# Moving the bias-row transposes and the gelu table load in a one-core Trainium2 kernel (gated mix of an SSM convolution and a token-mixing MLP)

## The chip, the cores and the metric

One core of a Trainium2 chip. The metric is the device time of one execution in microseconds (us); lower is better. The time before is the median of three runs. TensorE (PE) does the matmuls into PSUM, ScalarE (ACT) and VectorE (DVE) read PSUM and work on SBUF, GpSimd (POOL) and SyncE (SP) issue most of the DMAs.

## The reference

Two branches over S = 2048 positions and D = 640 channels, mixed by a gate per position. All inputs are bf16.

```python
x = A_q
g = sigmoid((x * gate_w).sum(-1, keepdims=True))
# a: a short causal convolution of k (4 taps a channel), times v; then a long causal
#    convolution over S with ssm_k, by FFT; plus the skip ssm_D; times q
kv = shift(k, shift_k) * v
a = x * (irfft(rfft(kv_padded) * rfft(ssm_k_padded))[:S] + kv * ssm_D)
# b: layernorm over D, then an MLP over the positions
h = layernorm(B-branch input x)
u = gelu(einsum("bsd,sf->bdf", h, w1) + b1)      # F = 1536
b = (einsum("bdf,fs->bds", u, w2) + b2).T
return g * a + (1 - g) * b
```

## The kernel before

The long convolution is done as matmuls with a 128x128 transform: `FTB` holds its cosine and sine tables, made at the start from integer ramps by ScalarE's sine. The whole kernel is one list of operations that `_Sched` gathers. `_Sched.add` finds what each operation depends on from the memory regions that it reads and writes; `_Sched.run` simulates the engines with a duration for each operation and a rate for each DMA, and from that picks the order on each engine and which of the four PSUM buffers (`pp`, each 1024 fp32 a partition) every group of matmuls takes; `emit` writes the operations out in that order. `_Tracker` puts in the semaphore waits. Every PSUM group is filled by TensorE (line 298) and drained by a step of another engine, nearly always ScalarE (`act`, line 676); the buffer is free for the next group when the drain has ended.

The stages that matter here, in order:

- **wtr / wT.** The SSM kernel rows (`ssm`) are turned by TensorE, eight 128x128 transposes to a buffer (five buffers for each half of the sequence), and drained into `wT`. In the first half, matmuls on a block of zeros (`zz`) stand between them.
- **W.** The transform of `wT`: groups of matmuls `pp<-wT,FTB` with 320 columns, drained to `C`. The first half has sixteen groups of four; the second begins with eight groups of two (`fwd_even`).
- **cst / cc.** `consts()` turns the rows of the two MLP biases (`rows`, loaded by two small DMAs from `B_b1` and `B_b2`) by five small matmuls against `ident`, and one activation drains them to `cc` (128x28). The gelu steps read their bias from it, and so does a VectorE step much later.
- **layernorm.** VectorE makes the statistics of `X` and scales it tile by tile; between these it copies the loaded rows of k (`kn` to `kp`), which SP's DMA then transposes into `KT`.
- **m1 / gelu.** The inner MLP product, `pp<-X,ring`: for each of 12 column blocks four runs of eight matmuls, drained by `GT <- gelu(pp + bias)`. Two blocks are open at a time; in the order before, the first two blocks' runs lie between the W groups. The first gelu makes ScalarE load another activation table.
- **kv.** The short convolution, `pp<-KF,KT` (matmuls of 128 or 96 columns), drained to `ksh`, multiplied by v on VectorE (`vkv`, `kv`).
- then the transform of kv, the products and mixing on VectorE (`C`, `SS`, `tm`), the rest of m1, the outer product m2 (`pp<-GT,W`), and the inverse transform (`pp<-C,FTB` and `pp<-SS,FTB`) with its drains `cgb`; the result goes out by `O`.

In the order of the profiled program, `cst` comes behind the third of the sixteen W groups, and `cc` behind the drains of two of them.

Of the kernel before, what the change touches and what calls it, by code (L numbers as in the profile page):

```python
# [13 lines left out]
ACT = mybir.ActivationFunctionType  # L14
ALU = mybir.AluOpType

ENGS = ("PE", "ACT", "DVE", "POOL")
# [294 lines left out]


class _Op:
    __slots__ = ("eng", "dur", "emit", "prio", "idx", "ndep", "succ", "vt", "vtrole", "end", "start", "kind", "lat", "deps", "name", "after", "nafter", "asucc", "lock")


class _VT:
# [10 lines left out]
class _Sched:  # L329
# [29 lines left out]
    def add(self, eng, dur, emit, reads, writes, prio=None, vt=None, lat=0.0, name=""):  # L359
        op = _Op()  # L360
        op.eng, op.dur, op.emit, op.lat, op.name = eng, dur, emit, lat, name
        op.idx = len(self.ops)
        op.prio = op.idx if prio is None else prio
        op.vt = vt
        op.lock = eng == "POOL"
        deps = set()
        self._conf(op, reads, "R", deps)
        self._conf(op, writes, "W", deps)
        if vt is not None:
            vt.left += 1  # L370
            if vt.last_pe is not None:
                deps.add(vt.last_pe)
            if eng == "PE":
                if vt.first is None:
                    vt.first = op
                vt.last_pe = op
            else:
                for d in deps:
                    if d.vt is not vt and not vt.keep:
                        if d not in vt.first.deps:  # L380
                            vt.first.deps.add(d)
        op.deps = deps
        op.after = set()
        self._rec(op, reads, "R")
        self._rec(op, writes, "W")
        self.ops.append(op)
        return op

    def run(self):
        ops = self.ops  # L390
        for op in ops:
            op.succ = []
            op.asucc = []
            op.ndep = len(op.deps) + len(op.after)
        for op in ops:
            for d in op.deps:
                d.succ.append(op)
            for d in op.after:
                d.asucc.append(op)
        engs = list(ENGS) + ["SP", "QA"]  # L400
        ready = {e: [] for e in engs}
        pend = {e: [] for e in engs}
        free = {"ACT": 2.93, "DVE": 0.85, "POOL": 0.83, "PE": 1.18, "SP": 0.0, "QA": 0.0}
        port = {"DVE": 0.0, "POOL": 0.0}
        dma_free = 0.3
        avail = {}
        for op in ops:
            avail[op] = 0.0
            if op.ndep == 0:
                heapq.heappush(pend[op.eng], (0.0, op.prio, op.idx))  # L410
        nfree = list(range(self.NSLOT))
        held = {}
        events = []
        order = []
        t = 0.0
        done = 0
        started = 0
        n = len(ops)
        frees = []
        while started < n:  # L420
            while frees and frees[0][0] <= t:
                _, sl, cls = heapq.heappop(frees)
                nfree.append(sl)
                held[cls] -= 1
            nxt = []
            progress = False
            for e in engs:
                while pend[e] and pend[e][0][0] <= t:
                    _, p, i = heapq.heappop(pend[e])
                    heapq.heappush(ready[e], (p, i))  # L430
                if free[e] > t:
                    nxt.append(free[e])
                    continue
                skipped = []
                pick = None
                while ready[e]:
                    p, i = heapq.heappop(ready[e])
                    op = ops[i]
                    if op.vt is not None and op.vt.slot is None:
                        c = op.vt.cls  # L440
                        if not nfree or held.get(c, 0) >= self.limit.get(c, 99):
                            skipped.append((p, i))
                            continue
                    pick = op
                    break
                for s in skipped:
                    heapq.heappush(ready[e], s)
                if pick is None:
                    if pend[e]:
                        nxt.append(pend[e][0][0])  # L450
                    continue
                op = pick
                progress = True
                started += 1
                if op.vt is not None and op.vt.slot is None:
                    op.vt.slot = nfree.pop(0)
                    held[op.vt.cls] = held.get(op.vt.cls, 0) + 1
                op.start = t
                if e in ("SP", "QA") or op.lat < 0:
                    issue = 1.2 if e == "POOL" else 0.1  # L460
                    s = max(t + issue, dma_free)
                    dma_free = s + op.dur
                    op.end = dma_free + 2.0 + (6.0 if e == "POOL" else 0.0)
                    free[e] = t + issue
                else:
                    op.end = t + op.dur
                    if op.lock:
                        op.end += max(port["POOL" if e == "DVE" else "DVE"] - t, 0.0)
                        port[e] = op.end
                    free[e] = op.end  # L470
                order.append(op)
                if op.vt is not None:
                    op.vt.left -= 1
                    if op.vt.left == 0:
                        heapq.heappush(frees, (op.end + 0.05, op.vt.slot, op.vt.cls))
                for s in op.asucc:
                    avail[s] = max(avail[s], op.start)
                    s.ndep -= 1
                    if s.ndep == 0:
                        heapq.heappush(pend[s.eng], (avail[s], s.prio, s.idx))  # L480
                for s in op.succ:
                    lat = 0.08 if s.eng == e else 0.15
                    if e == "PE" and s.eng == "PE":
                        lat = 0.0
                    avail[s] = max(avail[s], op.end + lat)
                    s.ndep -= 1
                    if s.ndep == 0:
                        heapq.heappush(pend[s.eng], (avail[s], s.prio, s.idx))
                nxt.append(free[e])
            if not progress:  # L490
                c = [x for x in nxt if x > t]
                if frees:
                    c.append(frees[0][0])
                assert c, "schedule stuck: " + str([(o.name, o.eng, o.ndep) for o in ops if not hasattr(o, "end")][:12])
                t = min(c)
        self.order = order
        self.makespan = max(o.end for o in ops)
        return order

    def emit(self):  # L500
        for op in self.order:
# [13 lines left out]
def _build(nc, A_q, A_k, A_v, A_shift_k, A_ssm_k, A_ssm_D, B_x, B_w1, B_b1, B_w2, B_b2, gate_w, out):  # L515
    Bsz, S, D = A_q.shape
    F = B_w1.shape[1]
# [8 lines left out]
    with ExitStack() as es:  # L526
# [8 lines left out]
        SC = _Sched(T, pp)  # L535
# [38 lines left out]
        gws = alloc("gws", [128, 1], F32)  # L574
# [64 lines left out]
        def ts(eng, o, a, s1, s2, op0, op1=None, mode=1, prio=None, extra=0.0):  # L639
            n = n_of(o)  # L640
            d = dve_dur(n, mode) + extra if eng == "DVE" else n / 900.0 + 0.2
            rr = [a] + [x for x in (s1, s2) if isinstance(x, bass.AP)]

            def f(e):
                if s2 is None:
                    return e.tensor_scalar(o, a, s1, None, op0=op0)
                return e.tensor_scalar(o, a, s1, s2, op0=op0, op1=op1)
            o_ = SC.add(eng, d, lambda s: T.op(eng, f, rr, [o]), rr, [o], prio=prio, name="ts")
            o_.lock = eng == "POOL" or mode > 1
            return o_  # L650

        def stt(eng, o, a, sc, b, op0, op1, acc=None, prio=None):
# [75 lines left out]
        def dr(t, off, ap):  # L728
            return bass.AP(tensor=t.tensor, offset=t.offset + off, ap=ap)
# [22 lines left out]
            dma(X[:, hk, :, :], dr(A_q, 512 * hk * D, [[4 * D, 128], [1, 4 * D]]), 128 * 5120, chain=True, rate=(352.0 if hk == 0 else 415.0))  # L752

        def w1_load(c, hk):
            dma(ring[c % 2][:, 4 * hk:4 * hk + 4, :], dr(B_w1, 512 * hk * F + 512 * c, [[4 * F, 128], [F, 4], [1, 512]]), 128 * 4096, chain=True)

        def k_load(hk):
            dma(kn[hk % 2][:, :, :], row8(A_k, hk), 128 * 5120, chain=True)
# [213 lines left out]
        for h in range(2):  # L972
            for db in range(ND):
                transp(h, db)
            if h == 0:
                consts()
            if h in (1,):
                fwd_even(srcW(h), h, C[h], 1.0 / 1024.0, h == 1, "W")
            for p in (PORD if h not in (1,) else PORD[2:]):
# [348 lines left out]
        Z1 = invmix(A1[0], A1[1], (SS, 0), False, [z0last])  # L1328
        inverse(1, Z1)

        SC.run()
        SC.emit()
        if _REPORT is not None:
            _REPORT(SC)
        T.wait_dma_final("SP", "out")

    return None


_REPORT = None  # L1340
# [1 line left out]
_INS = ['A_q', 'A_k', 'A_v', 'A_shift_k', 'A_ssm_k', 'A_ssm_D', 'B_x', 'B_w1', 'B_b1', 'B_w2', 'B_b2', 'gate_w']  # L1342
_OUTS = [((1, 2048, 640), 'bfloat16')]
# [23 lines left out]
```

## Time and profile before

| | |
|---|---|
| time, median of 3 runs | 179.74 us (179.69 to 180.02) |
| span of the profiled execution, first to last instruction | 178.7 us; the page lists no other time for it, and the median is 1.04 us above this span |
| TensorE busy | 170.9 us (96%), 1373 matmuls |
| VectorE busy | 169.5 us (95%) |
| ScalarE busy | 117.0 us (65%) |
| GpSimd busy | 43.1 us (24%) |
| mean granted TensorE clock | 0.999 |

"Busy" counts time in which an engine runs a compute instruction. A row of a timeline gives the start, the length from the first start to the last end, the engine and line, the operation, the tile written and the tiles read, shapes, and how many instructions are merged; the bracket is the idle time of that engine just before the row and what ended it. Neighbouring instructions of one engine overlap: a 320-column matmul is listed with about 0.30 us and the next starts 0.136 us after it. One line of the source stands for many places, since each kind of operation is recorded by one helper; the tiles tell them apart.

### The profile page before, as it was taken

What the parts mean: (1) busy time and instruction counts of PE and PEld (TensorE: products, weight loads), DVE (VectorE), ACT (ScalarE), POOL (GpSimd) and SP (SyncE); (2) the same over time, 40 slices, a digit from 0 to 9 for tenths busy, and PEclk for the clock granted to TensorE, in tenths of its full rate; (3) what the DMA queues carried; (4) which work ended last, traced back from release to release, by engine and by line L of the source; (5) the groups of instructions that cost most, each with busy time, mean ns of one, the idle gap of its engine ahead of it and who ended that gap; (6) DMA issues with size and microseconds to landing.
All of it is one profiled execution on the core that took longest, in us unless ns stands there. A gap on an engine that the chain in (4) does not pass through costs nothing.

```text
span 178.7 us, 3326 instructions
## 1 busy us (share of the span) xinstructions
PE 170.9 (96%) x1373; PEld 128.4 (72%) x1374; DVE 169.5 (95%) x203; ACT 117.0 (65%) x176; POOL 43.1 (24%) x52
## 2 busy tenths in 40 slices
PE   7868999899999999999999999999999999999993
PEld 2545787487778677776777778888888887777772
DVE  7799889979999999999999899999999999999984
ACT  4998997999899999428999921131231323753760
POOL 8099803100000065000241100403525000252000
PEclk9999999999999999999999999999999999999999
DMA  5999999999999999999499989797999999599463
GB/s 145 384 413 372 388 301 206 264 421 299 213 258 289 189 272 235 229 229 231 97 244 285 173 132 363 158 229 241 171 194 221 208 201 394 205 164 236 114 233 138
DMA packets 38542, 43.51 MB, mean 243 GB/s; under 512 B 15867, under 2 KB 31360, under 8 KB 38528
## 3 DMA queue, kind: packets, MB, share of 16 engines
q1 hardware_dynamic: 33296, 32.16, 59.1%
q0 software_dynamic: 5200, 11.14, 35.8%
q8 instruction: 11, 0.18, 0.4%
q14 instruction: 3, 0.02, 0.0%
q10 hardware_dynamic: 32, 0.01, 0.0%
HBM read 25.87 MB, written 2.62 MB: 159 GB/s over the span
## 4 chain that ended last, share of the span: by engine, by line
PE 88%; DMA 6%; ACT 3%; SPq 2%; issue 0%; DVE 0%
PE pp L298 88%; DMA rows<-in_B_b_dram 6%; SPq L272 2%; ACT C L676 1%; ACT L676 1%; ACT GT L676 0%; DVE O L688 0%
## 5 line engine op out<-in xcount | busy, mean ns | idle before, releaser
L632 DVE TENSOR_TENSOR C<-C 128x2560 bf16<-128x2560 bf16 (+2 forms) x37 | 54.5, 1525 | 1.1 <-ACT C L676 1.1
L298 PE MATMUL pp<-X,ring 128*128 128x320 bf16 x384 | 55.4, 299 | 0.0
L298 PE MATMUL pp<-GT,W 128*128 128x320 bf16 x384 | 52.6, 299 | 0.0
L298 PEld LDWEIGHTS pp<-GT,W 128*128 128x128 bf16 x384 | 43.6, 114 | 8.6
L298 PEld LDWEIGHTS pp<-X,ring 128*128 128x128 bf16 x384 | 37.3, 98 | 14.3
L676 ACT ACTIVATE C<-pp 128x640 bf16<-128x640 f32 x64 | 40.5, 737 | 3.2 <-PE pp L298 3.2
L676 ACT ACTIVATE O<-pp,c,omg 128x640 bf16<-128x640 f32 x15 | 13.3, 884 | 34.7 <-PE pp L298 34.7
L267 POOL DMA_DIRECT2D C<-C x8 | 11.0, 1615 | 45.0 <-DVE C L632 45.0
L298 PE MATMUL pp<-wT,FTB 128*128 128x320 bf16 x112 | 17.1, 299 | 1.4 <-ACT wT L676 0.8
L676 ACT ACTIVATE cgb<-pp,gg 128x640 bf16<-128x640 f32 x16 | 12.7, 794 | 5.7 <-PE pp L298 5.3
L676 ACT ACTIVATE GT<-pp,cc 128x640 bf16<-128x640 f32 x12 | 9.6, 801 | 9.0 <-PE pp L298 9.0
L298 PEld LDWEIGHTS pp<-wT,FTB 128*128 128x128 bf16 x112 | 10.5, 98 | 6.5 <-ACT wT L676 1.2
L945 DVE BATCH_NORM_STATS2 stats<-X 128x6 f32<-128x320 bf16 x32 | 13.5, 461 | 1.1 <-DMA X<-in_A_q_dram 1.1
L632 DVE TENSOR_TENSOR tm<-C,C 128x2560 bf16<-128x2560 bf16 (+1 forms) x7 | 14.3, 2060 | 0.0
L298 PE MATMUL pp<-C,FTB 128*128 128x320 bf16 x96 | 13.4, 299 | 0.0
L267 POOL DMA_DIRECT2D C<-q_hi x6 | 5.9, 977 | 27.6 <-DVE C L632 13.1
L298 PEld LDWEIGHTS pp<-C,FTB 128*128 128x128 bf16 x96 | 9.3, 98 | 3.8 <-issue 0.2
L676 ACT ACTIVATE gq<-gq 128x640 bf16<-128x640 bf16 x16 | 11.8, 739 | 0.1
L632 DVE TENSOR_TENSOR SS<-C 128x2560 bf16<-128x2560 bf16 x8 | 11.7, 1488 | 0.1
L632 DVE TENSOR_TENSOR C<-tm 128x2560 bf16<-128x2560 bf16 (+1 forms) x9 | 10.7, 1194 | 0.1
L676 ACT ACTIVATE ksh<-pp 128x1024 bf16<-128x1024 f32 (+1 forms) x12 | 9.9, 903 | 0.2 <-PE pp L298 0.2
L676 ACT ACTIVATE wT<-pp 128x1024 bf16<-128x1024 f32 x10 | 9.7, 1027 | 0.6 <-PE pp L298 0.6
(77 smaller groups left out, 188.8 us busy)
## 6 DMA issues: line engine op xcount, KB each, us to landing
ring<-in_B_w_dram SPq DMA_DIRECT2D x12, 512.0 KB, 9.6
W<-in_B_w_dram SPq DMA_DIRECT2D x12, 512.0 KB, 6.3
C<-C POOLq DMA_DIRECT2D x8, 640.0 KB, 10.6
X<-in_A_q_dram SPq DMA_DIRECT2D x4, 640.0 KB, 9.0
kn<-in_A_k_dram SPq DMA_DIRECT2D x4, 640.0 KB, 9.3
out_dram<-O SPq DMA_DIRECT2D x7, 320.0 KB, 3.2
C<-SS POOLq DMA_DIRECT2D x3, 640.0 KB, 11.7
ssm<-in_A_ssm_k_dram SPq DMA_DIRECT2D x3, 512.0 KB, 7.4
```

What stands on the lines that cost most here:

```text
L267: ins = engobj.dma_start(out_ap, in_ap, accum_op=ALU.add, max_dma_last_dim=2560)
L272: ins = engobj.dma_start(out_ap, in_ap)
L298: ins = self.nc.tensor.matmul(ps_ap, lhsT=lhsT, rhs=rhs, start=start, stop=stop, skip_group_check=True)
L632: o_ = SC.add(eng, d, lambda s: T.op(eng, lambda e: e.tensor_tensor(o, a, b, op), rd, [o]), rd, [o], prio=prio, name="tt")
L676: return T.op("ACT", lambda e: e.activation(o, src, func, **kw), rr + [src], ww)
L945: ops.append(SC.add("DVE", 0.38, (lambda o, i: lambda s: T.op("DVE", lambda e: e.bn_stats(o, i), [i], [o]))(o, i), [i], [o]))
```

## The change

The planner's run is taken out. The order of all operations and the PSUM buffer of each group are listed in the source (`_ORDER`, `_SLOTS`), and `follow` sets them. Against the order and buffers that the planner made in the kernel before:

- TensorE: the five `cst` transposes leave their place behind the third W group and stand before the last run of eight m1 matmuls ahead of the second half's W groups, that is between the two m1 runs that follow the last wtr group. Their buffer is the same one, number 1; the group before them in it is now the fourth `wtr` of the second half, the one behind them the first `fwd_even` W group.
- ScalarE: `cc` moves from behind the second drain of W to behind the fifth `wT` drain of the second half. Behind it stands a new activation, a gelu of one column of a constant (`cst[:,1:2]`, −0.5) into `gws`, which is written anew later. The load of the gelu table stands before this new activation, and no longer before the first gelu of the MLP.
- VectorE, GpSimd, SP and the DMAs issued by ScalarE keep their order, and every group keeps its buffer.

The other edits (a `hint` set in place of an added dependency, a DMA rate, a lock flag, the duration given to the new activation) were inputs of the planner.

```diff
-                        if d not in vt.first.deps:
-                            vt.first.deps.add(d)
+                        vt.first.hint.add(d)
...
-    def run(self):
...
+    def follow(self, order, slots):
+
+        vts, done = {}, set()
+        for op in self.ops:
+            if op.vt is not None and id(op.vt) not in vts:
+                vts[id(op.vt)] = op.vt
+        for vt, s in zip(vts.values(), slots):
+            vt.slot = s
+        self.order = [self.ops[i] for i in order]
+        assert len(set(order)) == len(self.ops)
+        for op in self.order:
+            assert all(d.idx in done for d in op.deps)
+            done.add(op.idx)
...
-            o_.lock = eng == "POOL" or mode > 1
+            o_.lock = eng == "POOL"
...
-            dma(ring[c % 2][:, 4 * hk:4 * hk + 4, :], ..., 128 * 4096, chain=True)
+            dma(ring[c % 2][:, 4 * hk:4 * hk + 4, :], ..., 128 * 4096, chain=True, rate=325.0)
...
             if h == 0:
                 consts()
+                act(gws[:, 0:1], cst[:, 1:2], ACT.Gelu_apprx_tanh, name="table").dur = 1.4
...
-        SC.run()
+        SC.follow([int(i) for i in _ORDER.split()], [int(i) for i in _SLOTS])
         SC.emit()
-        if _REPORT is not None:
-            _REPORT(SC)
...
+_ORDER = """
+2 0 3 1 4 5 6 7 8 9 10 18 15 11 12 19 16 13 20 14 17 30 21 33 22 31 23 32 24 36 34 25 26 35 27 57 38 28 37 29 242 39
...
+"""
+_SLOTS = "201301123023102310231021021010101031103103100310331003311023123123312311232302301231231232201230312031203120312031322032032020132013"
```

## The prediction

> **What bounds the kernel now.** I read the page's chain first, then the chain in order of time.
>
> ```profile
> ## 4 chain that ended last, share of the span: by engine, by line
> PE 88%; DMA 6%; ACT 3%; SPq 2%; issue 0%; DVE 0%
> PE pp L298 88%; DMA rows<-in_B_b_dram 6%; SPq L272 2%; ACT C L676 1%; ACT L676 1%; ACT GT L676 0%; DVE O L688 0%
> ```
>
> ```profile
> 4.64 10.14 DMA rows<-in_B_b_dram
> ...
> 14.82 16.34 PE pp L298 x143
> ...
> 32.50 1.28 ACT L676
> ...
> 33.80 0.79 ACT GT L676
> ...
> 35.92 140.11 PE pp L298 x1128
> ```
>
> From 35.92 us on, TensorE runs 1128 matmuls in a row to 176.03, and one VectorE step and one store follow. So the only question is when that run starts. Ahead of it the chain has two foreign pieces: the load of the bias rows, and ScalarE's table load (L676 without a tile) with the first gelu (GT). Both stall TensorE, as its timeline shows (start, length, what, count, idle time before it and what ended it):
>
> ```profile
> 12.47 1.67 PE L298 MATMUL pp<-wT,FTB 128*128 128x320 bf16 x11 [0.77 <-ACT wT L676]
> 14.82 0.38 PE L298 MATMUL pp<-ident,rows 4*128 4x4 bf16 x5 [0.68 <-DMA rows<-in_B_b_dram]
> 15.13 7.24 PE L298 MATMUL pp<-wT,FTB 128*128 128x320 bf16 x52
> ...
> 34.64 1.04 PE L298 MATMUL pp<-wT,FTB 128*128 128x320 bf16 x4 [0.51 <-ACT GT L676]
> 35.92 3.94 PE L298 MATMUL pp<-KF,KT 128*128 128x128 bf16 x72 [0.24 <-ACT C L676]
> ```
>
> ScalarE drains every PSUM buffer; its timeline shows the same stretch:
>
> ```profile
> 13.35 1.29 ACT L676 ACTIVATE C<-pp 128x640 bf16<-128x640 f32 x2
> 15.24 0.19 ACT L676 ACTIVATE cc<-pp 128x28 f32<-128x28 f32 x1 [0.60 <-PE pp L298]
> 15.33 8.45 ACT L676 ACTIVATE C<-pp 128x640 bf16<-128x640 f32 x14
> 23.99 4.69 ACT L676 ACTIVATE wT<-pp 128x1024 bf16<-128x1024 f32 x5 [0.20 <-PE pp L298]
> 29.55 1.30 ACT L676 ACTIVATE C<-pp 128x640 bf16<-128x640 f32 x2 [0.88 <-PE pp L298]
> ...
> 32.50 1.28 ACT L676 ACT_TABLE_LOAD   x1
> ```
>
> Last, two engines that could take over as the bound. GpSimd's copy out of KT (first row) runs as soon as the transpose of the k rows has landed; VectorE (next three) is filled from 37.00 on.
>
> ```profile
> 34.97 1.11 POOL L1079 COPY KT<-KT 128x20 bf16<-128x20 bf16 x1 [4.98 <-DMA KT<-kp]
> ```
>
> ```profile
> 23.91 0.80 DVE L647 TENSOR_SCALAR X<-X,mv,rstd 128x640 bf16<-128x640 bf16 x2
> ...
> 37.00 2.23 DVE L632 TENSOR_TENSOR C<-C 128x1280 bf16<-128x1280 bf16 x2 [1.05 <-ACT C L676]
> 39.37 1.49 DVE L632 TENSOR_TENSOR vkv<-ksh,vkv 128x2560 bf16<-128x2560 bf16 x1
> ```
>
> **The change part by part.** The list keeps every engine's order and every buffer, except this: the five transposes of the bias rows and their drain `cc` leave their place at 14.82 and 15.24. TensorE does the transposes ahead of the last eight matmuls of the X run at 26.90; ScalarE does `cc`, the table load and the tiny gelu behind its five wT drains, ahead of the drains at 29.55. The table load at 32.50 is gone. No DMA is moved, and the queues of SP, GpSimd and VectorE stand as before. Rates and locks are planner figures, which no longer plan anything. I follow TensorE's lead over the trace.
>
> 1. *Stall at 14.82.* The matmul starting at 13.84 is the twelfth; at 0.136 us a step the next could go at 13.98. Its buffer is that of the first W group, whose drain ends at 14.64 − 0.60 = 14.05, so it goes at 14.1. Then ScalarE paces: 14 drains in 8.45 are 0.60 each, four matmuls 0.54. ScalarE's pause of 0.60 and `cc` (0.10 to the next issue) fall away, drain k of the sixteen ends at 14.05 + 0.60(k − 1). The X matmuls at 22.21 use the thirteenth's buffer: 14.05 + 12 × 0.597 = 21.21, so 21.27. **Lead 0.94.** The sixteen drains end at 23.0, not 23.78.
>
> 2. *Second X group (24.78).* Its last two matmuls need the two tiles that VectorE ends at 24.71, and VectorE there waits for a load of k, not for TensorE. The group ends at 25.04 instead of 25.87. **Lead 0.83**, 0.87 at the next X run, where a wait of 0.05 for a wT drain vanishes.
>
> 3. *Transposes.* 14.82 to 15.13, 0.31 us of TensorE, are paid here again: nothing hides them. Their buffer's wT drain has ended by 26.83, before they start at 27.1. The W pair of 29.08 starts at 28.52. **Lead 0.56.**
>
> 4. *Table load.* The wT drains move up 0.94 and end at 27.74 instead of 28.68; `cc` to 27.83, load 1.28 to 29.13, the gelu of 128×1 at most the 0.20 of the 128×16 tanh (100.00). Next drain at 29.25 instead of 29.55. The 1.6 us put in exceed the old pause of 0.88; what pays is the lead of the wT drains. Queued behind it are four drains of W groups, for whose two buffers TensorE waits: the second is free at 30.55, TensorE came at 30.42. It loses 0.13 to 0.2; **lead 0.37**.
>
> 5. *First gelu.* Its matmuls end at 32.1 and no load stands before it: 32.17 to 32.96 instead of 33.80 to 34.59. The two remaining drains that KF×KT waits for end at 34.15; plus the 0.14 seen between drain and matmul at 35.92 it could start at **34.29, lead 1.63**.
>
> 6. *What is late next.* The second matmul of KF×KT reads the k transpose that GpSimd's row shows landed just before 34.97. That load hangs on a copy VectorE makes after a load of k; nothing in it moves. So the run starts effectively at 34.97, against 35.98 for the same matmul: **lead 1.0**, and TensorE rests 0.6 to 0.7 us instead.
>
> 7. *Does the lead last?* VectorE gets its last C drain by 35.4 and could resume at 35.87, ending the pair of 37.00 by 38.10; the next step waits for the third `ksh` drain, which follows KF×KT: 38.35 instead of 39.37. VectorE too gains 1.0. This matters: at 163.91 TensorE takes up C 0.11 us behind its own pace (158.36 + 40 × 0.136 = 163.80) because VectorE has just made it. VectorE's later pause (0.73 at 100.24) hangs on ScalarE, ScalarE on TensorE. Later DMAs all follow one of these engines.
>
> Sum: −1.0 on a span of 178.7. The page gives the span alone; the median, 179.74, is 1.04 above it, for what lies around. 179.74 − 1.0 = **178.74**. Bounds of unknown prices: the gelu of one column between 0 and the 0.29 of the smallest GpSimd step on three columns (29.70) moves step 4 alone, and 0.68 of rest in step 6 covers it. The TensorE lead from step 1, between 0 and 0.94, is covered likewise down to 0.3.
>
> At step 4 a rule speaks against the change. The Trainium skill (ScalarE: Activation LUTs, What ACT_TABLE_LOAD costs) puts a switch at about 1283 ns of load plus 1380 ns of drain, 2.66 us. The trace agrees on the load, 1.28, but shows no drain: the load starts 0.02 after one activation ends and the next starts 0.01 after the load. By the page's sum the time would be that of the second rival. I go by the row.
>
> **The rivals.**
>
> *The k transpose comes earlier than in this one profile.* Then TensorE starts at up to 34.29, and VectorE becomes the bound: 38.10 against 39.37, 1.27. Time 178.47. For it: this landing had a second of slack, so nothing has measured its scatter. Against: loads of k and v queue back to back.
>
> *ScalarE is held twice as long at the load.* Another 1.28 puts the four drains at 30.53; waits for their buffers follow at both W pairs, the gelu ends at 34.24, the last needed drain at 35.43, KF×KT starts at 35.58: gain 0.34, time 179.40. Against: the 0.02 and 0.01 around the present load. This is the one that the Trainium skill's 2.66 us amounts to.
>
> *The transpose comes later.* The gain shrinks one for one with its landing and is gone at 35.92: 179.5 to 179.74. It is hidden today, so it may scatter.
>
> *Slower: the new rest costs TensorE its clock.* The seven 128x512 matmuls at 1.18 took 3.16 us, near 0.43 each against 0.22 at 11.19: half rate at the start. If the rest before KF×KT brought that back for as long, it would cost some 1.6 us: 180.3. It decides from the length of the rest: pauses of 0.77 and 0.68 left the granted clock at 1.00 in the windows around them, and the new one is 0.7 at most.
>
> That the change does not do what it says is excluded by the two orders, which differ only as told.
>
> **How the numbers follow.** Forecast 0.78, earlier 0.06, held twice 0.05, later 0.06, slower 0.05. A measurement tells about 0.2%, 0.36 us, from no change: faster is below 179.38. The held case lies on that line and is split: faster 0.78 + 0.06 + 0.03 = 0.87, same 0.06 + 0.02 = 0.08, slower 0.05. The range runs from the earlier case, 178.4, to 179.3, a transpose half a microsecond late; held, the rest of later and slower, 0.16 or less, stay outside.
>
> **What would show it.** Right: no wait for `rows`; X at 21.3; one gelu table load near 27.8; gelu at 32.2; KF×KT waiting for DMA KT until about 35.0, VectorE's vkv step at 38.35; from there the same 141 us. Wrong at step 6 if KF×KT waits for ScalarE; at step 7 if a wait of TensorE for VectorE opens at 149.7 or 163.9 and swallows the lead; at step 4 if more than 0.1 us stands idle around the load.

## The result, and the profile after

| | before | after |
|---|---|---|
| time, median of 8 runs each | 179.84 us (179.54 to 180.40) | 179.31 us (178.94 to 179.75) |
| ratio, 95% interval | | 0.9967 [0.9953, 0.9981] |
| profiled execution: span | 178.7 us | 177.5 us |
| profiled execution: time | not listed | 179.46 us |

The change makes the kernel faster by 0.53 us, some 0.3%; the interval puts it between 0.34 and 0.85 us. The forecast was 178.74 with a range up to 179.3: the sign is right, the gain is half of what was expected, and the time lies at the upper end of the range, 0.01 us beyond it. Two more measurements of the same kernel, e8 and e12 below, gave 0.998 [0.9962, 0.9999] and 0.9987 [0.9969, 1.0006]; over the three the gain is about 0.4 us.

In the one profiled execution, nearly every step is where the prediction put it. The page's chain, and the chain in order of time:

```profile
PE 79%; DMA 14%; DVE 5%; issue 1%; SPq 0%
PE pp L298 79%; DMA kn<-in_A_k_dram 6%; DMA KT<-kp 4%; DMA X<-in_A_q_dram 3%; DVE stats L848 3%; DVE X L550 1%; SPq L272 0%; DVE kp L667 0%; DVE mv L852 0%; DVE O L591 0%
```

```profile
27.93 6.71 DMA KT<-kp
34.64 0.05 issue
34.69 140.08 PE pp L298 x1127
```

`rows` and ScalarE's table load are gone from the chain; ahead of the long TensorE run stands the transpose of the k rows (`KT<-kp`). TensorE's timeline (start, length, what, count, idle before and what ended it):

```profile
11.95 8.92 PE L298 MATMUL pp<-wT,FTB 128*128 128x320 bf16 x63 [0.77 <-ACT wT L579]
20.80 1.25 PE L298 MATMUL pp<-X,ring 128*128 128x320 bf16 x8
...
26.75 0.32 PE L298 MATMUL pp<-ident,rows 4*128 4x4 bf16 x5
...
33.80 0.22 PE L298 MATMUL pp<-KF,KT 128*128 128x128 bf16 x1
34.69 3.90 PE L298 MATMUL pp<-KF,KT 128*128 128x96 bf16 x71 [0.67 <-DMA KT<-kp]
```

The 63 W matmuls run without a stop, the transposes stand at 26.75 without a wait, and the second KF×KT matmul waits 0.67 us for the transpose. ScalarE's timeline over the same stretch:

```profile
22.58 4.69 ACT L579 ACTIVATE wT<-pp 128x1024 bf16<-128x1024 f32 x5
27.11 0.24 ACT L579 ACTIVATE cc<-pp 128x28 f32<-128x28 f32 x1
27.37 1.28 ACT L579 ACT_TABLE_LOAD   x1
28.66 0.20 ACT L579 ACTIVATE gws<-cst 128x1 f32<-128x1 f32 x1
28.77 2.73 ACT L579 ACTIVATE C<-pp 128x640 bf16<-128x640 f32 x4
31.68 0.80 ACT L579 ACTIVATE GT<-pp,cc 128x640 bf16<-128x640 f32 x1 [0.18 <-PE pp L298]
```

The load sits behind the wT drains with 0.02 and 0.01 us around it, and the first gelu now waits for TensorE, not for a table. VectorE and GpSimd at the same place:

```profile
33.26 4.35 DVE L535 TENSOR_TENSOR C<-C 128x1280 bf16<-128x1280 bf16 x4
38.09 1.49 DVE L535 TENSOR_TENSOR vkv<-ksh,vkv 128x2560 bf16<-128x2560 bf16 x1 [0.48 <-ACT ksh L579]
```

```profile
34.70 3.05 POOL L983 COPY KT<-KT 128x20 bf16<-128x20 bf16 x1 [5.18 <-DMA KT<-kp]
```

VectorE rests 0.48 us before `vkv`, so it is not the bound here.

### The profile page after: what moved, and what is told of

Its sections match the earlier page's. It is cut to its first block, busy times and chain, and to the rows that moved or that the text cites. A ratio compares the mean times of both kernels' runs of the same rounds, so it can differ in the third digit from the quotient of the medians.

```text
span 177.5 us, 3328 instructions
## 1 busy us (share of the span) xinstructions
PE 171.6 (97%) x1373; PEld 128.4 (72%) x1374; DVE 169.5 (95%) x203; ACT 116.8 (66%) x177; POOL 45.0 (25%) x52
## 4 chain that ended last, share of the span: by engine, by line
PE 79%; DMA 14%; DVE 5%; issue 1%; SPq 0%
PE pp L298 79%; DMA kn<-in_A_k_dram 6%; DMA KT<-kp 4%; DMA X<-in_A_q_dram 3%; DVE stats L848 3%; DVE X L550 1%; SPq L272 0%; DVE kp L667 0%; DVE mv L852 0%; DVE O L591 0%
## 5 line engine op out<-in xcount | busy, mean ns | idle before, releaser
L267 POOL DMA_DIRECT2D O<-q_hi x4 | 4.8, 1200 | 21.3 <-DVE q_hi L535 21.3
## 6 DMA issues: line engine op xcount, KB each, us to landing
C<-C POOLq DMA_DIRECT2D x8, 640.0 KB, 10.9
C<-SS POOLq DMA_DIRECT2D x3, 640.0 KB, 12.6
```

The lines of the kernel that those rows point to most:

```text
L267: ins = engobj.dma_start(out_ap, in_ap, accum_op=ALU.add, max_dma_last_dim=2560)
```

## The experiments

Two readings stood against each other. **Theory A** (the prediction's): the run of KF×KT sets the time; before, ScalarE's drains behind the table load released it; after, the second k transpose does. **Theory B**: the gain is that of the removed wait for `rows`. A third question came with the size: why 0.5 us, when the long TensorE run ends 1.26 us earlier in the trace of after (174.77) than in that of before (176.03).

Edits are given in operation numbers of the list `_ORDER`: 9 and 10 load the bias rows, 48 and 49 the first two pieces of the k rows, 14 and 51 quarters of w1, 52 the gate row `gwb`, 180 and 182 are the first two k transposes, 67 is `cst`, 68 `cc`, 69 the tiny gelu, 253 the first load of w1 behind the later k transposes. "Before's order" is the list written out from the kernel before, without 69. A line that begins with `SP:` gives SP's part of the list alone.

**e1, the transposes alone.**

```diff
-                act(gws[:, 0:1], cst[:, 1:2], ACT.Gelu_apprx_tanh, name="table").dur = 1.4
```

> The five bias transposes and cc stand where the change puts them; there is no tiny gelu, so the table load stays before the first MLP gelu. Theory (KF x KT starts at the later of ScalarE's last needed drain and the landing of the second k transpose): by the steps of the prediction the lead at that point is 0.56 us, the landing does not bind, 0.4 to 0.6 us faster than before. Rival (the transposes' wait is hidden by the drains of the W groups, only the table load matters): 0.0 to 0.1 us faster, and TensorE would show new waits for ScalarE between 14 and 22 us that use up the 0.68.

**e2, the table load alone:** before's order, with 69 behind the fifth wT drain (200). The edit is shown against the changed kernel; 67 and 68 go back to their old places.

```diff
-... 73 123 122 124 76 ... 162 384 67 248 ... 164 200 68 69 168 ...
+... 73 123 67 122 124 68 76 ... 162 384 248 ... 164 200 69 168 ...
```

> The transposes and cc stay in their old place; only the tiny gelu with the table load is put behind the fifth wT drain. Theory: the load overruns the pause, the second W pair's buffer is late by 0.44, but the first MLP gelu no longer waits for the load: lead 0.8 us before KF x KT, not yet bound by the landing; 0.5 to 0.8 us faster than before, so that the two parts alone add up to more than the whole change gives. Rival (a switch costs 2.66 us, as the long sum has it): no gain or slower, with idle time around the load.

Measured: e1 179.90 against 180.06, 0.9989 [0.9974, 1.0003], which can't be told from no change; e2 179.70, 0.9977 [0.996, 0.9995], 0.4 us. TensorE's timelines, of e1 and then of e2:

```profile
24.28 0.80 PE L298 MATMUL pp<-X,ring 128*128 128x320 bf16 x4 [0.18 <-DVE X L550]
...
33.99 1.04 PE L298 MATMUL pp<-wT,FTB 128*128 128x320 bf16 x4 [0.51 <-ACT GT L579]
35.27 3.94 PE L298 MATMUL pp<-KF,KT 128*128 128x128 bf16 x72 [0.24 <-ACT C L579]
```

```profile
13.98 0.38 PE L298 MATMUL pp<-ident,rows 4*128 4x4 bf16 x5 [0.41 <-DMA rows<-in_B_b_dram]
...
34.29 0.22 PE L298 MATMUL pp<-KF,KT 128*128 128x128 bf16 x1
35.03 3.90 PE L298 MATMUL pp<-KF,KT 128*128 128x96 bf16 x71 [0.53 <-DMA KT<-kp]
```

With the table load left in its place (e1) the gelu and the drains still release KF×KT, as before, and part of the lead from the early stretch is lost at the second X group, which waits 0.18 for VectorE's tiles behind the k load. With the load moved and the wait for `rows` kept (e2), the run waits for the transpose just as in the whole change. So in the traces it is the table load that moves the release of the run, and taking away the wait for `rows` alone (e1) leaves ScalarE in charge of it. The times alone don't settle it: e1 and e2 lie 0.2 us apart and their intervals overlap. Both missed what was expected of them, e1 with 0.16 us for 0.4 to 0.6, e2 with 0.36 for 0.5 to 0.8; e2 was also expected not to meet the transpose yet.

**e3, the k rows loaded earlier, in the changed kernel; e4, the same move in before's order.**

```diff
-SP: 13 14 48 49 50 51 52 180 182
+SP: 13 48 14 49 50 51 52 180 182
```

> The changed kernel with one DMA moved: the load of the first block of k rows stands before the load of the second quarter of the first MLP weights, instead of behind it. The first k transpose can then be issued some 1.2 us earlier, the second lands near 33.4 us instead of 34.6. Theory: the landing is what binds the changed kernel, so KF x KT follows to about 33.9, and VectorE (0.48 us of rest before vkv) becomes the bound: another 0.4 to 0.6 us faster than the changed kernel. Rival (the lead is limited elsewhere, by ScalarE or later): the same time as the changed kernel.

> The kernel before with that one DMA moved and nothing else. Theory: there the landing is hidden by a second or less behind ScalarE's drains, so it is worth nothing: within 0.2 us of before. Rival (k rows bind the kernel before as well): 0.4 us or more faster than before.

Measured: e3 179.46, 0.9966 [0.9947, 0.9985], the same as the change itself; e4 179.69, 0.9973 [0.995, 0.9996]. e3 was expected to bring 0.4 to 0.6 us more. SP's timeline shows why it doesn't, first after, then e3 (the length is that of both issues together; the issue is the time in which the transpose holds SP's queue):

```profile
23.57 7.47 SPq L265 DMA_TRANSPOSE KT<-kp  x2
```

```profile
22.58 8.60 SPq L265 DMA_TRANSPOSE KT<-kp  x2
```

The first block of k rows was ready earlier and SP began the first transpose 0.99 us sooner, but issuing the two took 1.13 us longer: they were through at 31.04 and 31.18, and the transpose landed at 34.64 (after, above) and in e3 no sooner, since TensorE waited for it until 34.77. What stands ahead in SP's queue fits both. In after the last load ahead, the gate row, was issued at 16.78 and landed 10.9 us later, at 27.69, and the second issue began at 27.93, with the first just through:

```profile
16.78 4.34 SPq L272 DMA_DIRECT2D gwb<-in_gate_w_dram  x1
...
27.93 3.11 SPq L265 DMA_TRANSPOSE KT<-kp  x1
```

In e3 the gate row landed at 27.88, and the second issue began at 28.05. e4's small gain is a miss: in its trace KF×KT waits for ScalarE as before, nothing shows a transpose at work. Its trace has no stall at the second X group, where e1 and e7 have one; that would fit a k load that comes sooner, but e6's trace, with the k load in its old place, has none either, so e4's gain stays unexplained.

**e5, the gate row loaded later, in the changed kernel; e6, the same in before's order.**

```diff
-SP: 50 51 52 180 182 ... 252 253
+SP: 50 51 180 182 ... 252 52 253
```

> The changed kernel with the load of the gate row (gwb, 160 KB, first used after 59 us) moved behind the last k transposes in SP's queue. In the six traces so far the second k transpose landed 6.8 to 7.0 us after the gate row, whatever the k rows did, so the theory is now: KF x KT of the changed kernel hangs on what stands ahead of the transposes in the DMA queue, not on the k rows. It then lands 0.5 us earlier (gwb came 0.5 us behind the load before it), TensorE follows to the 0.48 us that VectorE has left: 0.4 to 0.5 us faster than the changed kernel, 0.9 to 1.1 faster than before. Rival (the landing hangs on the k rows, and the move of those failed for another reason): the same time as the changed kernel.

> The kernel before with only that load moved. Theory: KF x KT waits for ScalarE's drains there, so an earlier landing is worth nothing: within 0.2 us of before, although the trace shows the transpose landing 0.5 us earlier. Rival (the queue delays something else as well): 0.4 us or more faster.

**e7, the bias rows loaded earlier, in before's order; e8, the change once more beside them.**

```diff
-SP: 6 7 8 9 10
+SP: 6 9 10 7 8
```

> The kernel before with the two small loads of the bias rows moved ahead of the last two loads of X in SP's queue, and nothing else: the wait at 14.82 us by itself. Traces that keep the old place of the transposes showed this wait at 0.68, 0.41 and 0 us, so it scatters from execution to execution with the landing of the loads. Theory: its mean is 0.3 to 0.4 and not the 0.68 of the one profile; this kernel gains 0.1 to 0.35 us, about as much as moving the transposes alone did (0.2). Rival (0.68 is typical): 0.55 us or more.

> The changed kernel again, beside the others on the same chip: 0.4 to 0.8 us faster than before; its KF x KT waits for the transpose, and its span stays below the 178.7 us of the profiled execution of before by 0.9 us or more, while the median of the executions of before has a span near 178.1.

Measured against 179.87: e5 179.30, 0.9971 [0.9945, 0.9996]; e6 180.12, 1.0013 [0.9992, 1.0035]; e7 179.86, 1.0003 [0.9981, 1.0026]; e8 179.62, 0.998 [0.9962, 0.9999]. e5 is not told from e8; in its trace the transpose landed no sooner than in the others, and TensorE waited for it until 35.05. e8's own gain, 0.25 us, is below the 0.4 to 0.8 expected. e6 is the test of theory A from the other side; it came out 0.25 us slower, where within 0.2 was expected, and its interval includes no change. SP's and TensorE's timelines of e6:

```profile
23.57 6.96 SPq L265 DMA_TRANSPOSE KT<-kp  x2
```

```profile
34.77 3.94 PE L298 MATMUL pp<-KF,KT 128*128 128x128 bf16 x72 [0.24 <-ACT C L579]
```

The issues end at 30.53, and GpSimd's copy, which waits for the landing alone, starts at 34.1. In before it started at 34.97, but the loads ahead had landed later there too; reckoned from the landing of the last quarter of w1, the transpose landed after 6.8 us in e6 and after 7.4 in before and e1. A transpose that lands half a microsecond sooner is worth nothing as long as ScalarE releases the run, here at 34.77. e7 takes the wait for `rows` away without touching the order of the engines, and shows no gain, where 0.1 to 0.35 us was expected; its interval leaves room for 0.34. Its trace of TensorE shows where a lead goes:

```profile
13.52 0.32 PE L298 MATMUL pp<-ident,rows 4*128 4x4 bf16 x5
...
24.45 0.80 PE L298 MATMUL pp<-X,ring 128*128 128x320 bf16 x4 [0.33 <-DVE X L550]
```

**e9, both moves in the changed kernel; e10, the last quarter of w1 besides; e11, e10's moves in before's order; e12, the change once more.**

```diff
-SP: 13 14 48 49 50 51 52 180 182 ... 252 253
+SP: 13 48 14 49 50 51 180 182 ... 252 52 253      (e9)
+SP: 13 48 14 49 50 180 51 182 ... 252 52 253      (e10, e11)
```

> The changed kernel with both DMA moves: the first k rows ahead of the second quarter of the first MLP weights, the gate row behind the last k transposes. Each alone left the landing of the second k transpose near 34.7 to 35.0 us, because SP's issue of the first transpose did not end before the loads queued ahead of it had landed. Theory (the landing binds the changed kernel, and the queue ahead of the transposes sets it): with both, the issue of the first ends near 27.4, the second lands near 34.0, KF x KT starts at 34.0 to 34.4: 0.2 to 0.5 us faster than the changed kernel. Rival (something else holds the run at 34.7): the same.

> As the run before it, and the last quarter of the first MLP weights (512 KB, used from 30.4 us) is put between the two k transposes. Theory: the first transpose is issued by 26.5, the second lands near 33.2, ahead of ScalarE's drains, so that KF x KT no longer waits for a DMA; VectorE, which had 0.3 to 0.5 us of rest before vkv, becomes the bound: 0.3 to 0.5 us faster than the changed kernel. If the weights land after 30.4 that is given back. Rival as before: the same time.

> The kernel before with the same three DMA moves. Theory: KF x KT waits there for ScalarE, not for the transpose, so the same earlier landing is worth nothing: within 0.25 us of before. Rival (the earlier landing is worth the same in both kernels): 0.3 to 0.5 us faster than before.

> The changed kernel beside the three others: 0.3 to 0.7 us faster than before, KF x KT waiting for the transpose, which lands between 34.6 and 35.0 us.

Measured against 179.98: **e9 178.90, 0.994 [0.9921, 0.996]**, the fastest version, 1.08 us under the kernel before and 0.61 under e12; e10 179.87, 0.999 [0.9972, 1.0008]; e11 180.18, 1.0008 [0.9981, 1.0035]; e12 179.51, 0.9987 [0.9969, 1.0006]. e9's timelines, SP and then TensorE:

```profile
22.49 8.42 SPq L265 DMA_TRANSPOSE KT<-kp  x2
```

```profile
33.88 0.22 PE L298 MATMUL pp<-KF,KT 128*128 128x128 bf16 x1
34.52 3.90 PE L298 MATMUL pp<-KF,KT 128*128 128x96 bf16 x71 [0.43 <-DMA KT<-kp]
```

In e9 the issues are through at 30.91, 0.13 us sooner than after. This one execution took 179.26, 0.36 above e9's median, and its transpose landed at 34.48, where e12's landed at 34.46; so it does not show where the typical one gains. By the working below, the run would start near 34.2 there. Which of the two moves carries the gain is not shown. e10's timelines, SP and then TensorE, and the end of its chain:

```profile
26.53 0.59 SPq L272 DMA_DIRECT2D ring<-in_B_w_dram  x1
27.17 4.63 SPq L265 DMA_TRANSPOSE KT<-kp  x1
```

```profile
31.61 1.26 PE L298 MATMUL pp<-X,ring 128*128 128x320 bf16 x8 [1.08 <-DMA ring<-in_B_w_dram]
...
35.03 4.25 PE L298 MATMUL pp<-KF,KT 128*128 128x128 bf16 x72
```

```profile
27.17 8.16 DMA KT<-kp
35.34 0.04 issue
35.38 140.07 PE pp L298 x1127
```

e10 gives back what e9 gained, in two ways. The weights put between the transposes land late, and m1 waits 1.08 us for them. The second transpose stands behind these weights in the queue: its issue ends at 31.80, after they have landed, and it lands at 35.34, 0.70 later than after. The second is the one that its chain runs through. e11's transpose landed late in the same way (its GpSimd copy started at 35.60), so e11 is no second test of an earlier landing.

## Why the prediction was right in its steps and wrong in its size

Set against the profile of before, the changed kernel's early stretch starts 0.52 us sooner (W at 11.95, not 12.47), for a reason outside the change: its first loads landed sooner. With 0.52 added to the times of after:

| step | predicted | after, plus 0.52 |
|---|---|---|
| 1: X run | 21.27 | 21.32 |
| 3: W pair behind the transposes | 28.52 | 28.62 |
| 4: table load | 27.83 to 29.13 | 27.89 to 29.17 |
| 4: next drain | 29.25 | 29.29 |
| 5: first gelu | 32.17 | 32.20 |
| 5: first KF×KT matmul | 34.29 | 34.32 |

1. **Steps 1 to 5 held**, to 0.1 us. Behind the second X group of step 2 the next matmuls started at 24.59, with 0.52 added 25.11, against 25.04 predicted.
2. **Step 6 held in what it said of time, and its reason was wrong.** The run starts at 34.69 against 34.97 predicted (35.21 with the 0.52 added), released by the transpose. But the landing is not set by VectorE's copies. Each copy must end before SP can issue its transpose, and the first issue did start 0.03 us behind the first copy; yet in e3 that copy was ready a microsecond sooner and the landing stayed, and the second copy, ready at 25.4 in both, was done 2.5 us before the second issue began. The landing follows the end of SP's second issue, some 3.5 to 3.6 us ahead of it in 13 of the 14 traces (31.04 to 34.64 in after; 2.2 in e7). And the issue follows the loads queued ahead. In all 14 traces the first issue ended 0.1 to 0.4 us after the last load queued ahead of it had landed (27.88 after 27.69 in after), whether that was the gate row or a quarter of w1. This match in time held through every edit; what in the queue makes it so is open.
3. **Step 7 held.** From the second KF×KT matmul to the last matmul's end lie 140.04 to 140.09 us in all 14 traces, of every version. The start of that run is the time.
4. **The mis-sized term is the base of the sum: "1.04 above it, for what lies around".** The runs list span and time of each execution, and the time lies 1.8 to 2.0 us above the span, 1.9 at the median (in after 179.46 − 177.5 = 1.96). So the profiled execution of before, span 178.7, took about 180.6 by this reckoning (its own time is not listed), not 179.74: it was a late one. The 35 executions of before beside e1 to e4 have a median span of 178.2, and the one among them with a span of 178.7 took 180.66. The forecast of the span, 178.7 − 1.0 = 177.7, was good (177.5); taken with the 1.9 around, it is 179.6 for that execution, whose time before was 180.6. That the measured median still fell at the edge of the range is luck: the range reached up to 179.3 for the sake of a late transpose, not for this.
5. **What the gain is on the median.** Of a time, 1.91 lies around the span, 2.70 between the last matmul's end and the span's end, and 140.05 is the run: 144.66 in all. A time of 179.84 to 180.06 before then means a run that starts at 35.18 to 35.40, not 35.98; 179.31 to 179.62 after means 34.65 to 34.96, where the traces show the transpose. The traces bear this out. Where ScalarE releases the run, its second matmul started at 35.98 (before) and 35.92 (e11), both with late first loads and a wait for `rows`, and at 34.82 to 35.32 in e1, e4, e6 and e7; where the transpose releases it, at 34.51 to 35.05 (e10, which delays it, apart). Step 1's 0.68 is such a scattering term too: in traces with the transposes in the old place the wait was 0.41 (e2), 0.47 (e11), and nothing in e4 and e6; in e7 the load itself was moved. A lead taken there runs into the second X group's wait for VectorE (0.18 in e1, 0.33 in e7).

The rivals: *held twice as long* is refuted by the 0.02 and 0.01 around the load. The Trainium skill (ScalarE: Activation LUTs, What ACT_TABLE_LOAD costs) counts 1380 ns of drain beside the load; no run here shows it, and the measurement decides. *The clock lost in the new rest* is refuted: after 0.67 of rest, 71 matmuls took 3.90 us, against 72 in 3.94 before, at a granted clock of 1.00 (33 to 40 us). The clock is listed as 1.00 in the first 5 us of before too, so the slow matmuls that gave this rival its price are not shown to be a matter of the clock. *The transpose later* is half of what happened, seen from the median: not that it came late, but that the drains it replaces typically come 0.6 to 0.8 us sooner than in the one profile. *The transpose earlier* was not met by the change itself; e9 aimed at it and gained, but its one trace does not show the earlier landing.

## What to carry to other kernels

A profile is one execution. Before its span is used as the base of a sum, set its own time (span plus what lies around it, which other runs of the kernel show) beside the median; a wait that hangs on the first loads may be worth its full length in that execution and nothing in the typical one. When two releasers stand close to each other ahead of the same run, the gain of removing one is the distance to the other, and moving only the other, as e6 did, brings nothing. And a load that is moved must be followed to who reads it and to what stands behind it in the queue: e10's weights came late for m1 and held the second transpose.

## What the runs showed of the hardware

- SP's issue of a k transpose takes 3.1 to 5.4 us of SP's queue (second and first issue of e3), and starting it sooner only made the first one longer. It ended 0.1 to 0.4 us after the last load queued ahead had landed (27.88 after 27.69 in after; in e10, where a load stood ahead of the second transpose too, 31.80 after 31.56).
- GpSimd's copy of 128x20 took 1.11 us before, 3.05 after and 0.84 in e3. No wait in these three traces is put down to it.
- The first loads land in two groups about half a microsecond apart: TensorE's run of W behind its wait for a wT drain started at 11.9 to 12.0 in nine of the traces and at 12.4 to 12.6 in the other five (before, e3, e5, e8, e11), whatever the kernel. That alone is as large as the change.
